# The kv product and its product with Wo, head by head on small TensorE tiles, with Wo loaded by quadrants behind the z row

## Chip, cores, metric

One core of one Trainium2 chip. The metric is the device time of the whole program in microseconds (us). A program runs several times on one chip, in turns with the kernel before; medians are quoted, and every ratio is the mean time of one kernel's fast runs over that of the other's fast runs of the same rounds, so it is not quite the ratio of the medians. The runs of one kernel in one group span 0.6 to 2.8 us here, mostly 1 to 2. The effects below are of that size, so each one is also read from the trace, in stretches of a few us, where times repeat to hundredths (the two kv blocks take 1.79 us each in before and again in b_plus64).

Names in the profile: PE is TensorE's matmul, PEld its weight load (each matmul has one of its own: 4083 of each in before), DVE is VectorE, ACT ScalarE, SPq the queue of SyncE that issues the transfers. All instructions carry the line of one helper, L176, so pieces are told apart by their tiles: `ps<-g,wv` is the kv product, `ps<-wo,kvt` its product with Wo, `ps<-pk,xres` the G product before them, `ps<-mw,pqt` the attention output after them, `ps<-pqt,zsel` the denominator.

## The reference, cut

```python
def _A_ref(x, wqkv, wo):                 # x: 1 x 2048 x 1024, H = 32 heads of Dh = 32
    q, k, v = ...                        # x @ wqkv, split by heads
    phi = lambda t: jnp.where(t > 0, t + 1, jnp.exp(t)) + 1e-06
    pq, pk = (phi(q), phi(k))
    kv = jnp.einsum('bhsd,bhse->bhde', pk, v)          # one 32 x 32 block per head
    z = jnp.einsum('bhsd->bhd', pk)
    num = jnp.einsum('bhqd,bhde->bhqe', pq, kv)
    den = jnp.einsum('bhqd,bhd->bhq', pq, z)[..., None] + 1e-06
    return (num / den) ... @ wo

h = _layernorm(x) * (1 + ca) + sa        # modulation from silu(c) @ w_mod
x = x + ga * _A_ref(h, A_wqkv, A_wo)
# ... second layer norm, then the gated feed-forward block (70% of the time, untouched here)
```

The kernel never forms v. It computes G = (modulated x) transposed times phi(k), with a rank-one term that needs the z row (the sum of phi(k)); then kv transposed = Wv transposed times G per head, then M = kv times Wo per head, and the output is phi(q)/den times M.

## The kernel before: the parts touched

```python
P.dma("wo", WO[:], wov)                      # 2 MB in one transfer, ahead of everything below

def g_group(g):                              # 16 groups of 16 matmuls 128x512, five PSUM banks in turn
    ...
def g_evac(g):                               # ACT scales a row of ZB (needs the z row), DVE evicts the bank into G
    ...

def z_row():
    ...                                      # two matmuls, a copy, then out to DRAM and back, broadcast
    zw = P.dma("zw", ZDR[0].rearrange("(g p) -> g p", p=128), ZR8[0:NHG, :])
    P.wait_for("sp", [zw])
    P.dma("zr", ZB[:], ZDR[0:1, :].to_broadcast([128, D]))

def kvt_mm(half):                            # four groups of four heads
    for hl in range(4):
        hg = 4 * half + hl
        for dt in range(NDT):
            P.pe("matmul", out=PS[:, 6, hl * 128:(hl + 1) * 128], lhsT=WV[:, dt, hg * 128:(hg + 1) * 128],
                 rhs=G[:, dt, hg * 128:(hg + 1) * 128], start=(hl == 0 and dt == 0), stop=(dt == NDT - 1), ...)
    P.dve("tensor_tensor", out=KVT[:, 4 * half:4 * half + 4, :], in0=PS[:, 6, :]..., in1=MASK..., op=ALU.mult)

def m_mm(hg, banks):                         # a block-diagonal 128x128 times Wo, two halves of 512 columns
    for nh in range(2):
        ...
        P.pe("matmul", out=PS[:, bank, :], lhsT=KVT[:, hg, :], rhs=WO[:, hg, nh * 512:(nh + 1) * 512], ...)
        ...                                  # evicted to MW by ACT and DVE in turn

# order: G groups 0..10, kvt_mm(0), G 11, m_mm(0), G 12, m_mm(1), G 13, m_mm(2), G 14, m_mm(3), G 15,
# six output matmuls, kvt_mm(1), five, m_mm(4), two, m_mm(5), two, m_mm(6), one, m_mm(7), then output matmuls only
```

In each 128x128 block of `kvt_mm` only four 32x32 blocks on the diagonal are wanted; the mask throws the other twelve away, and `m_mm` multiplies by their zeros.

## Time and profile before

| | before |
|---|---|
| median of 3 runs | 831.1 us (830.98 to 831.93) |
| span of the profiled run | 829.4 us |
| TensorE busy | 823.2 us, 99% |
| kv product | 64 matmuls 128x128, two blocks of 1.79 us |
| kv with Wo | 16 matmuls 128x512, eight pairs of 0.43 us |

The chain that ended last is TensorE for 97% of the span. Listed in order of time it runs from 20.93 us for 805.88 us through nothing but matmuls. So, by this chain, only TensorE's own time counts, and a new stop of TensorE counts in full.

TensorE's groups by form (count, then busy us and mean ns of one, then idle time before):

```profile
L176 PE MATMUL ps<-wo,kvt 128*128 128x512 bf16 x16 | 4.8, 379 | 0.0
L176 PE MATMUL ps<-g,wv 128*128 128x128 bf16 x64 | 3.9, 219 | 0.0
L176 PE MATMUL ps<-pqt,zsel 128*32 128x512 bf16 x32 | 1.9, 380 | 0.0
```

The mean of 379 ns is one matmul from its start to its modelled end; successive ones overlap (they start 216 ns apart), so costs are taken from starts. TensorE's timeline around the touched pieces (start, length, count):

```profile
130.24 3.62 PE L176 MATMUL ps<-pk,xres 128*128 128x512 bf16 x16
133.79 1.91 PE L176 MATMUL ps<-pqt,zsel 128*32 128x512 bf16 x32
...
166.72 1.95 PE L176 MATMUL ps<-g,wv 128*128 128x128 bf16 x32
168.51 3.62 PE L176 MATMUL ps<-pk,xres 128*128 128x512 bf16 x16
171.96 0.59 PE L176 MATMUL ps<-wo,kvt 128*128 128x512 bf16 x2
172.40 3.62 PE L176 MATMUL ps<-pk,xres 128*128 128x512 bf16 x16
...
188.80 1.95 PE L176 MATMUL ps<-g,wv 128*128 128x128 bf16 x32
190.59 1.24 PE L176 MATMUL ps<-mw,pqt 128*128 128x512 bf16 x5
```

The kv block starts at 166.72 and the next G group at 168.51: 1.79 us for 32 matmuls, 56 ns each. A pair of kv-with-Wo matmuls takes 0.43 us (171.964 to 172.395, unrounded). Together these pieces are 2 x 1.79 + 8 x 0.43 = 7.0 us, 0.85% of the span. The denominator's 32 matmuls show what narrow tiles can do: 32 columns each, four at a time, eight rounds in 1.84 us.

The transfer queue, and ACT's first use of the z row:

```profile
131.35 1.29 SPq L176 DMA_DIRECT2D wo<-in_A_wo_dram  x1
132.68 0.53 SPq L176 DMA_DIRECT2D z_row<-zr  x1
140.08 0.33 SPq L176 DMA_DIRECT2D zb<-z_row  x1
```

```profile
144.12 1.33 ACT L176 ACTIVATE gtmp<-zb,modcol 128x512 f32<-128x512 f32 x2 [16.09 <-DMA zb<-z_row]
```

The z row's write is issued behind Wo's 2 MB, and its read back comes 7.4 us later; ACT waits until 144.12. TensorE still does not stop: it comes back to the first of its five banks at 146.0, and DVE had freed that at 145.6.

### The profile page before, as it was taken

The numbers are of one execution on the slowest core, as the hardware profiler recorded it, in microseconds if no ns is written. First come the engines' busy times: TensorE is split into PE (matmuls) and PEld (weight loads), VectorE is DVE, ScalarE is ACT, GpSimd is POOL, SyncE is SP. The second block draws the span as 40 slices with busy tenths as digits, with TensorE's granted clock in tenths as the row PEclk, the third lists the DMA queues.
The fourth block names the chain that finished last, engine by engine and source line by source line (L and its number), as shares of the span: only waits on it lengthen the run. The fifth ranks groups of instructions, "written<-read, shape, count | busy, mean of one in ns | idle before, by whom it ended". The sixth has DMA issues, their size and how long they took to land.

```text
span 829.4 us, 10017 instructions
## 1 busy us (share of the span) xinstructions
PE 823.2 (99%) x4083; PEld 378.8 (46%) x4083; DVE 312.6 (38%) x665; ACT 197.5 (24%) x336; POOL 39.9 (5%) x57
## 2 busy tenths in 40 slices
PE   8999999999999999999999999999999999999998
PEld 4544444444444444444444444444444444444444
DVE  5797986756955521121221112122111211221111
ACT  4757641323242111011111101111110111111011
POOL 1010000000130000030000003000000300000000
PEclk9999999999999999999999999999999999999999
DMA  9969656938397985700455571045557004553000
GB/s 321 287 151 231 148 159 171 201 104 304 60 256 229 276 264 158 192 25 15 124 155 150 153 185 33 16 124 153 154 151 190 26 18 123 154 152 87 0 26 26
DMA packets 199246, 119.28 MB, mean 144 GB/s; under 512 B 57881, under 2 KB 182945, under 8 KB 199201
## 3 DMA queue, kind: packets, MB, share of 16 engines
q1 hardware_dynamic: 199184, 118.65, 52.8%
q8 instruction: 32, 0.52, 0.3%
q14 instruction: 14, 0.11, 0.0%
q10 hardware_dynamic: 16, 0.00, 0.0%
HBM read 100.67 MB, written 4.33 MB: 127 GB/s over the span
## 4 chain that ended last, share of the span: by engine, by line
PE 97%; DMA 2%; SPq 1%; issue 0%; DVE 0%
PE ps L176 97%; DMA wsa<-in_w_mod_dram 2%; SPq L176 1%; DVE xres L176 0%
## 5 line engine op out<-in xcount | busy, mean ns | idle before, releaser
L176 PE MATMUL ps<-h2t,gug 128*128 128x512 bf16 x896 | 211.7, 379 | 0.0
L176 PE MATMUL ps<-h2t,guu 128*128 128x512 bf16 x896 | 211.7, 379 | 0.0
L176 DVE TENSOR_TENSOR at<-sg,ps 128x512 bf16<-128x512 bf16 x112 | 77.0, 687 | 282.8 <-PE ps L176 281.2
L176 ACT ACTIVATE sg<-ps 128x512 bf16<-128x512 f32 x112 | 66.9, 597 | 309.7 <-PE ps L176 309.7
L176 PEld LDWEIGHTS ps<-h2t,guu 128*128 128x128 bf16 x896 | 87.6, 98 | 105.7
L176 PEld LDWEIGHTS ps<-h2t,gug 128*128 128x128 bf16 x896 | 87.7, 98 | 105.5
L176 PE MATMUL ps<-wd_a,at 128*128 128x512 bf16 (+1 forms) x512 | 112.4, 377 | 0.0
L176 PE MATMUL ps<-ht,wqk 128*128 128x512 bf16 x512 | 111.7, 379 | 0.0
L176 PE MATMUL ps<-wd_b,at 128*128 128x512 bf16 (+1 forms) x384 | 85.0, 377 | 0.0
L176 PEld LDWEIGHTS ps<-wd_a,at 128*128 128x128 bf16 x512 | 50.1, 98 | 59.6
L176 DVE TENSOR_TENSOR ut<-att,gb_b 128x512 bf16<-128x512 bf16 (+1 forms) x32 | 14.3, 447 | 166.8 <-ACT att L176 166.8
L176 PEld LDWEIGHTS ps<-ht,wqk 128*128 128x128 bf16 x512 | 49.5, 98 | 58.7 <-DVE biasq L176 0.2
L176 ACT ACTIVATE att<-ps 128x512 bf16<-128x512 f32 (+1 forms) x32 | 17.4, 591 | 182.1 <-PE ps L176 182.1
L176 PEld LDWEIGHTS ps<-wd_b,at 128*128 128x128 bf16 x384 | 37.6, 98 | 44.7
L176 PE MATMUL ps<-pk,xres 128*128 128x512 bf16 x256 | 56.5, 379 | 0.0
L176 PE MATMUL ps<-mw,pqt 128*128 128x512 bf16 x256 | 56.3, 379 | 0.0
L176 POOL TENSOR_SCALAR h2t<-h2t,modcol 128x512 bf16<-128x512 bf16 x32 | 26.3, 836 | 383.4 <-DMA h2t<-xn 383.4
L176 ACT ACTIVATE e<-ps 128x512 bf16<-128x512 f32 x56 | 33.1, 603 | 31.7 <-PE ps L176 19.8
L176 PEld LDWEIGHTS ps<-mw,pqt 128*128 128x128 bf16 x256 | 24.9, 98 | 30.2 <-DVE xres L176 0.4
L176 PEld LDWEIGHTS ps<-pk,xres 128*128 128x128 bf16 x256 | 24.9, 98 | 29.9 <-issue 0.4
L176 ACT ACTIVATE junk<-xres 128x1024 bf16<-128x1024 bf16 x24 | 25.4, 1058 | 35.1 <-DVE xres L176 34.9
L176 DVE SCALAR_TENSOR_TENSOR xres<-ps,xres 128x512 bf16<-128x512 f32 x32 | 21.4, 688 | 12.3 <-PE ps L176 11.5
(107 smaller groups left out, 344.8 us busy)
## 6 DMA issues: line engine op xcount, KB each, us to landing
gug<-in_B_w_gate_dram SPq DMA_DIRECT2D x56, 512.0 KB, 4.0
guu<-in_B_w_up_dram SPq DMA_DIRECT2D x56, 512.0 KB, 5.3
xres<-in_A_x_dram SPq DMA_DIRECT2D x20, 256.0 KB, 7.7
rb<-recip_den SPq DMA_DIRECT2D x8, 512.0 KB, 11.5
stgx<-in_w_mod_dram SPq DMA_DIRECT2D x2, 2048.0 KB, 7.9
wd_a<-in_B_w_down_dram SPq DMA_DIRECT2D x4, 1024.0 KB, 7.8
out_dram<-xres SPq DMA_DIRECT2D x31, 128.0 KB, 1.7
xres<-in_A_x_dram SPq DMA_DIRECT2D x3, 1024.0 KB, 14.1
```

The lines of the kernel that those rows point to most:

```text
L176: return getattr(e, method)(**kw)
```

## The change

Its intent is to compute only the wanted blocks. A head's kv is a matmul with 32 columns of weights, so four heads (one of each group) are put side by side in four column tiles, as the denominator's matmuls are in before, where four start 3 to 4 ns apart and the next four 206 to 216 ns later. kv with Wo needs 32 rows and 32 columns, so 16 heads are put in sixteen 32 by 32 tiles: group g takes row tile g and PSUM bank g, head h takes column tile h. For that, the change lays Wo's rows in another order in SBUF, with eight transfers (two groups of four quadrants, no waits between the four). They are issued behind the z row. The eviction of kv needs no mask. In numbers: 64 matmuls become 256, 16 become 64.

```diff
-        wov = A_wo.rearrange("(kt p) n -> p kt n", p=128)
+        wov = A_wo.rearrange("(f g h e) n -> f g e h n", f=2, g=4, h=4)
-        P.dma("wo", WO[:], wov)
+        def wo_load(f):
+            outs = [WO[32 * g:32 * g + 32, 4 * f:4 * f + 4, :] for g in range(4)]
+            def fn(e, outs=outs, f=f):
+                return [e.dma_start(out=o_, in_=wov[f, g]) for g, o_ in enumerate(outs)]
+            P.add("sp", fn, reads=[], writes=outs, lane="wo%d" % f, ninc=4, tag="wo")
...
         def kvt_mm(half):
+            for h in range(4):
                 for dt in range(NDT):
+                    for g in range(4):
+                        c0 = 512 * half + 128 * g + 32 * h
+                        P.pe("matmul", out=PS[32 * g:32 * g + 32, 6, 32 * h:32 * h + 32], lhsT=WV[:, dt, c0:c0 + 32],
+                             rhs=G[:, dt, c0:c0 + 32], start=(h == 0 and dt == 0), stop=(dt == NDT - 1), ...)
+            P.dve("tensor_copy", out=KVT[:, half, :], in_=PS[:, 6, 0:128])
+
+        def m_mm(half, nh, banks):
+            for k in range(4):
+                for g in range(4):
+                    h = (g + k) % 4
+                    P.pe("matmul", out=PS[32 * h:32 * h + 32, banks[g], :],
+                         lhsT=KVT[32 * g:32 * g + 32, half, 32 * h:32 * h + 32],
+                         rhs=WO[32 * g:32 * g + 32, 4 * half + h, nh * 512:(nh + 1) * 512], ...)
+            # four evictions to MW, two on ACT and two on DVE
...
             if g == 0:
                 z_row()
+                for f in range(2):
+                    wo_load(f)
...
-            if 11 <= g < 15:
-                m_mm(g - 11, [MB, 7])
+            if 11 <= g < 13:
+                m_mm(0, g - 11, [MB, 7, G_BANKS[4], 6])
...
         kvt_mm(1)
         wo_part(0, 1, range(2, 4))
-        # three output matmuls, m_mm(4), two, m_mm(5), two, m_mm(6), one, m_mm(7)      [summarised]
+        wo_part(1, 0, range(1))
+        m_mm(1, 0, [4, 5, 7, 6])
+        wo_part(1, 0, range(1, 4))
+        wo_part(1, 1, range(4))
+        m_mm(1, 1, [4, 5, 7, 6])
```

Left out: the smaller KVT tile, one G group moved to another bank, and the order of the first two row tiles of the output.

## The prediction

> **What bounds it now.** TensorE. The chain of waits runs through TensorE without a gap from 20.9 to 826.8 us (97% of the span); granted clock 1.0. Only TensorE time can be gained. The groups by form show the two touched pieces: `ps<-g,wv` 64 matmuls 128x128, `ps<-wo,kvt` 16 matmuls 128x512. In the timeline of TensorE the two kv blocks start at 166.72 and 188.80 and last 1.79 us each (32 at 56 ns); the kv-with-Wo matmuls come in eight pairs of 0.43 us (216 ns each), 3.45 us in all. Together 7.0 us: the ceiling.

> **What changes.** Only a 32 by 32 block per head is useful; the rest was masked. After: 256 matmuls of N=32 in four column tiles, 64 of N=512 in sixteen 32 by 32 tiles.

> The trace has a model: the denominator's 32 matmuls, 32 columns wide, N=512, at 133.79 us. Each four start 3 to 4 ns apart and the next four 206 to 216 ns later: four tiles for one streaming time [...]. Entering and leaving costs: the last full-array matmul starts 309 ns before the first tiled one, and 312 ns pass at the end, against 216: about 0.1 us each way [...].

> Estimates from these:
> - kv: 64 rounds of four. N=1 load-and-matmul pairs (the modulation columns) follow every 25 ns here; eight instructions at 3.4 ns are 27 ns. At 28 ns a round a block takes 0.9 + 0.2 us of switching, not 1.79: saves 0.7, twice = 1.4 us.
> - kv with Wo: a block of 16 tiles takes about 0.216 + 0.07 of issue + 0.2 switching = 0.5 us, not 0.86 (four full matmuls): saves 0.36, four times = 1.45 us.
> - New waits: the second half's second block reuses all four banks after 7 matmuls (1.5 us), while each of ACT and DVE has two evictions (0.60 and 0.69 us) plus latency: 0.1 to 0.2 us lost. The KVT copy before the third block (0.3 us) is about covered by three matmuls (0.65 us).

> **Off the critical path.** The z row now goes before Wo's 2 MB: before, its broadcast was issued at 140.1 (7 us after its write, queued behind Wo) and ACT waited for it until 144.1. I expect it near 137. G's evictions then start right after the reciprocal (about 141.6, not 144.9); TensorE did not wait there, so this gains 0. Wo in eight 256 KB loads lands near 145 to 148; the fold by the gate needs it at 150. The reciprocals may be a microsecond or two late; DVE has that to spare.

> **Sum.** 831.1 - 2.7 = 828.4 us; range 826.8 to 830.4. Faster by over 2%: 0.01; within 2%: 0.98; slower: 0.01.

> **What would show it.** kv blocks of about 1.1 us from start to the next full-array matmul; kv-with-Wo blocks of about 0.5 us; TensorE still without idle time between 126 and 200 us except a few tenths before the last block; `zb` landing before 140.

> **What would make it wrong.** If small matmuls on different column tiles do not overlap, and each pair costs 25 ns, a kv block (128 pairs) takes 3.2 us and the kernel gets about 1.5 us slower. If sixteen tiles writing four banks do not run at once, the Wo gain vanishes. Switching rows and columns could cost more than 0.1 us. If Wo or the reciprocals land microseconds late, DVE delays kv and TensorE idles.

## More of the kernel before

The page's chain of waits (by engine, then by line) and its line of queue 8:

```profile
PE 97%; DMA 2%; SPq 1%; issue 0%; DVE 0%
q8 instruction: 32, 0.52, 0.3%
```

## The result and the profile after

| | before | after |
|---|---|---|
| median | 831.41 us (4 runs) | 829.94 us (4 runs, 829.23 to 830.76) |
| ratio of fast runs | | 0.9982, 95% interval 0.9965 to 1.0 |
| span of the profiled run | 829.4 us | 827.4 us |

The gain is 1.5 us where 2.7 were predicted. The interval reaches 1.0, so the time alone would not settle that there is a gain; a second group (after_again, below) has 0.9984, with 0.9971 to 0.9998. The measured time lies inside the predicted range, but over a microsecond of the expected gain is missing. In this trace 79 of the 4323 matmul records are missing (their weight loads are all there), which breaks the chain of waits into 206 pieces; the timeline is read instead, with the weight loads where a matmul is missing.

The groups by form, then TensorE's timeline over the same stretch:

```profile
L176 PE MATMUL ps<-g,wv 128*32 128x32 bf16 x256 | 2.5, 182 | 0.0
L176 PE MATMUL ps<-wo,kvt 32*32 32x512 bf16 x64 | 1.7, 385 | 0.0
```

```profile
187.11 1.19 PE L176 MATMUL ps<-g,wv 128*32 128x32 bf16 x128
188.47 0.59 PE L176 MATMUL ps<-mw,pqt 128*128 128x512 bf16 x2 [0.16 <-issue]
188.99 0.43 PE L176 MATMUL ps<-wo,kvt 32*32 32x512 bf16 x16
189.36 1.68 PE L176 MATMUL ps<-mw,pqt 128*128 128x512 bf16 x7
190.97 0.43 PE L176 MATMUL ps<-wo,kvt 32*32 32x512 bf16 x16
191.34 1.04 PE L176 MATMUL ps<-mw,pqt 128*128 128x512 bf16 x4
193.41 2.96 PE L176 MATMUL ps<-mw,pqt 128*128 128x512 bf16 x12 [1.03 <-issue]
```

Both products got cheaper as planned: a kv-with-Wo block takes 191.34 - 190.97 = 0.37 us and the switch into it 0.09 more. But after the last of them TensorE makes four matmuls, and then stops for a microsecond. The releaser named is "issue", which means that the profile shows nothing that it waited for. (The 0.16 at 188.47 is a matmul whose record is missing.) The weight loads, of which none is missing, give the stop exactly, with the spacing to the one before:

```
weight load 1370 (counting from 0)   191.999 us   +0.216
weight load 1371                     193.407 us   +1.408     no semaphore on it
weight load 1372                     193.622 us   +0.215
```

The matmul of load 1370 already waits: its record starts at 193.406, so the stop lies between a weight load and its own matmul. So 1.408 - 0.216 = 1.19 us are lost in the one place. Without it the change would have gained about 2.6 us.

The transfer queue, ACT, and queue 8:

```profile
130.71 1.16 SPq L176 DMA_DIRECT2D z_row<-zr  x1
133.46 0.33 SPq L176 DMA_DIRECT2D zb<-z_row  x1
133.83 4.33 SPq L902 DMA_DIRECT2D wo<-in_A_wo_dram  x8
```

```profile
138.17 1.33 ACT L176 ACTIVATE gtmp<-zb,modcol 128x512 f32<-128x512 f32 x2 [10.68 <-DMA zb<-z_row]
q8 instruction: 34, 0.56, 0.3%
```

- **Theory A, instruction supply.** TensorE reached the seam between two blocks before the second had arrived. (That the second is asked for at about the time when TensorE enters the first was the author's assumption here.)
- **Theory B, a data wait** on ACT or DVE that the profile does not name. The first residual addition on DVE ended at 193.42, just as TensorE resumed.
- **Theory C, something that follows the change of tile mode.**

By A, a seam lies at a fixed count of instructions from the start of the program. B and C are tied to a place in the work. That makes them easy to tell apart: shift the work against the count.

### The profile page after: what moved, and what is told of

It is laid out like the page before. It is cut to its first block, busy times and chain, and to the rows that moved or that the text cites. A ratio compares the mean times of both kernels' runs of the same rounds, so it can differ in the third digit from the quotient of the medians.

```text
span 827.4 us, 10429 instructions
## 1 busy us (share of the span) xinstructions
PE 816.5 (99%) x4244; PEld 376.4 (45%) x4323; DVE 311.3 (38%) x665; ACT 197.4 (24%) x336; POOL 39.8 (5%) x57
## 4 chain that ended last, share of the span: by engine, by line
PE 96%; DVE 2%; issue 1%; DMA 0%; ACT 0%; DVEq 0%; ACTq 0%
PE ps L176 96%; DVE acc L176 1%; DMA xres<-in_A_x_dram 0%; DVE stats L176 0%; DVE pkt L176 0%; DVE e L176 0%; ACT xres L176 0%; DVE pqt L176 0%; ACT e L176 0%; DVE mv L176 0%; DVE xres L176 0%; DVE ht L176 0%; DVE ve L176 0%; DVE nmr L176 0%; DVEq L247 0%
```

## The experiments

Eleven runs were made in three groups (after_again and best_again repeat a kernel); a group shares its chip and its runs of the kernel before. All gave the right result except quiet_dma, which is wrong.

| run | median us | before, same chip | ratio, 95% interval | where TensorE stopped |
|---|---|---|---|---|
| a_plus64 | 828.94 | 831.55 | 0.9970 (0.9958 to 0.9983) | nowhere |
| a_plus16 | 833.41 | 831.55 | 1.0020 (1.0006 to 1.0034) | loads 1115 and 1371 |
| half0 | 829.82 | 831.55 | 0.9980 (0.9968 to 0.9993) | nowhere |
| b_plus64 | 832.75 | 831.55 | 1.0013 (1.0001 to 1.0026) | G, for the z row |
| after_again | 829.79 | 831.23 | 0.9984 (0.9971 to 0.9998) | load 1371 |
| z_first | 831.49 | 831.23 | 1.0004 (0.9991 to 1.0016) | nowhere |
| half1 | 834.57 | 831.23 | 1.0035 (1.0023 to 1.0048) | load 1243 |
| kv_only | 830.34 | 831.23 | 0.9990 (0.9977 to 1.0002) | nowhere |
| best_again | 828.76 | 831.57 | 0.9969 (0.9956 to 0.9981) | nowhere |
| best_wo_first | 834.97 | 831.57 | 1.0046 (1.0032 to 1.0059) | G, for the z row |
| quiet_dma | 829.33 (one run) | 831.57 | none | load 1115 |

Timed runs were five for each but quiet_dma, all in the fast state; quiet_dma has one look of unknown state.

### a_plus64: the work shifted by 64 pairs

```diff
-        warm(13, bank=3)
+        for _ in range(77):
+            P.pe("matmul", out=PS[:, 3, 0:86], lhsT=IDENT[:], rhs=E1[:, 0, 0:86], start=True, stop=True)
```

These are filler matmuls at the start of the kernel (its helper is named `warm`), there before and after the change; 77 short ones stream as many columns as the 13 long ones (6622 and 6656). In the trace of after the 13 start 426 to 427 ns apart (401 at the first step, 357 at the last), and the five of the same shape that follow from 8.66 us start 215 to 216 ns apart.

> The kernel after, with the 13 clock-warming matmuls of 512 columns at the start replaced by 77 of 86 columns: the same streaming, 64 more load-and-matmul pairs ahead of everything, so all later instructions lie half a 16 KB instruction block further on. Theory A (TensorE's instruction stream ran dry at 192.2 us after the kv block had used 256 instructions in 1.1 us; the stall sits at the seam of two fetched blocks, the 1371st weight load): the seam leaves the critical place, the 1.2 us gap is gone from the profile, and the time is about 1.2 us below after, near 828.8 us, ratio to before 0.9965 to 0.9972. Theory B (the gap is a wait for data of ACT or DVE that the profile does not name, such as the first residual addition, which ended as TensorE resumed): the program is the same from there on, the gap stays at the same matmul with about 1.2 us, time as after, ratio 0.998. Theory C (a delay that follows the change of tile mode): as B.

Measured: 828.94 us, ratio 0.9970, and no stop. TensorE's timeline at the same place:

```profile
191.55 0.43 PE L176 MATMUL ps<-wo,kvt 32*32 32x512 bf16 x16
191.92 1.25 PE L176 MATMUL ps<-mw,pqt 128*128 128x512 bf16 x5
```

The weight loads run on at 0.216 us through the place where the gap was. Theories B and C do not expect this: the work, its waits and its tile modes are the same here. (In the control b_plus64, below, some transfers ran a microsecond later with the new warming, so it is a_plus16 and half1 that put B and C out.) This trace has all its matmuls, so the true prices are read from it, each from the end of the last full matmul's 216 ns to the start of the next full one:

| block | before | a_plus64 | saved |
|---|---|---|---|
| first kv block | 1.79 us | 1.29 us | 0.50 |
| second kv block | 1.79 us | 1.22 us | 0.57 |
| kv with Wo, each of four | 0.86 us (two pairs) | 0.46 us | 0.40 |
| sum | | | 2.67 |

The time gained is 831.55 - 828.94 = 2.61 us, so the sum closes, and more closely than the noise of the runs would lead one to expect.

### a_plus16: shifted the wrong way

The same edit with 29 matmuls of 229 columns.

> The same with 29 warming matmuls of 229 columns: 16 more pairs. Theory A: the seam stays at the 1371st weight load, which is now 16 loads earlier in the program, inside the last kv-with-Wo block, reached 1.1 us earlier, while its fetch is asked for at most 0.2 us earlier: a gap of about 2 us, at another matmul than in after; time 0.7 to 1.0 us above after, about 830.8 us, ratio to before 0.999 to 1.0. Theories B and C: the gap at the same matmul of the program, 1.2 us, ratio 0.998.

Measured: 833.41 us, and the stop is at weight load 1371 again, though that is now in the middle of the last kv-with-Wo block:

```profile
190.53 1.68 PE L176 MATMUL ps<-mw,pqt 128*128 128x512 bf16 x7
192.14 0.39 PE L176 MATMUL ps<-wo,kvt 32*32 32x512 bf16 x4
194.70 0.49 PE L176 MATMUL ps<-wo,kvt 32*32 32x512 bf16 x12 [2.17 <-issue]
195.12 1.46 PE L176 MATMUL ps<-mw,pqt 128*128 128x512 bf16 x3
```

Sixteen independent matmuls are cut after the record of the fourth. Loads are 2.55 us apart where 3 ns is usual. The place by count stayed, the place in the work moved, as A alone says. The time missed the expectation of about 830.8 us. Two things were not expected: a second stop of 0.76 us at load 1115, just 256 loads earlier, in the first half's first kv-with-Wo block; and a slow clock after the long stop, with matmuls 427 ns apart in place of 216 for some eight of them, 1.6 us more (the mean granted clock of this execution is 0.998, in after 1.0). With those the time adds up: 828.8 (after without a stop) + 2.5 + 0.8 + 1.6 = 833.7.

### half0 and half1: one half of the heads each

The change applied to the first half alone and to the second half alone; the other half has its matmuls, Wo layout and order of before.

```diff
+            if f == 1:                       # half0; f == 0 in half1
+                P.dma("wof", WO[:, 4 * f:4 * f + 4, :], wof[:, 4 * f:4 * f + 4, :])
+                return
...
-        kvt_mm(1)                            # half0
+        kvt_full(1)                          # and its order of before; half1 does so for half 0
```

> The change for the first half of the heads only; the second half has its 128 by 128 matmuls, Wo layout and order of before. From the trace of after, the first half's kv block saves about 0.47 us and its two kv-with-Wo blocks 0.40 us each: 1.27 us. Theory A: no burst in the second half, no gap: 1.2 to 1.3 us below before, about 830.1 us, ratio 0.9985, so as good as or little worse than the whole change. Theory B: the gap belongs to the order of the second half (two tiles of rows taken together), which is undone, so it predicts the same here; C: a gap of some tenths may follow the first half's blocks.

Measured for half0: ratio 0.9980, 1.7 us below before, no stop. The trace has the kv block at 1.29 and the two kv-with-Wo blocks at 0.46 us, as in a_plus64. Half of the change is worth as much as the whole as it was made.

> The change for the second half of the heads only, the first half as before. By the sum of parts without stalls it saves 0.56 + 0.8 = 1.36 us. Theory A: the seams of instruction blocks lay at weight loads 1115 and 1371 (a_plus16), so one lies at 1243; here it falls into the last kv-with-Wo block (loads 1230 to 1245), 167 loads after the kv block's start at 1076, of which 128 run in 1.1 us: a gap of 2 to 2.6 us there, likely with a slow clock after it as in a_plus16, and a time of 1 to 3 us ABOVE before, so 832.5 to 834.5 us. Theories B and C (data wait, mode switching) expect the gain of 1.36 less about 1.2: ratio 0.9998.

Measured for half1: 834.57 us, 3.3 us ABOVE before, and the stop exactly where the count puts it, at weight load 1243:

```profile
193.05 0.42 PE L176 MATMUL ps<-wo,kvs 32*32 32x512 bf16 x12
196.23 0.40 PE L176 MATMUL ps<-wo,kvs 32*32 32x512 bf16 x4 [2.76 <-issue]
```

The loads are 3.15 us apart, a longer stop than the 2 to 2.6 us expected, and the matmuls after it are again 427 ns apart for some microseconds (mean granted clock 0.998). This was the hardest test of A, because by the work alone half1 should have gained 1.36 us. The seams found so far, 1115, 1243 and 1371, are 128 loads apart: one block of 256 instructions each.

### b_plus64: a control that moved

The kernel before with the warming of a_plus64.

> Control: the kernel before with the same 77 short warming matmuls. Before has no gap, and its kv blocks use 64 instructions in 1.8 us, so all theories expect ratio 1.000, within 0.0005, and no gap; if it moves by more, the warming itself changed the time and a_plus64 has to be read against this one.

Measured: 1.0013, 1.2 us slower. TensorE stopped in the G groups:

```profile
146.70 4.49 PE L176 MATMUL ps<-pk,xres 128*128 128x512 bf16 x20 [0.49 <-DVE g L176]
```

Here the z row's read back was issued at 141.14, one us later than in before, so DVE's first eviction came too late for the sixth G group; 0.66 us were lost between the first G group and the first kv block (40.70 us from load to load, before 40.04). The margin of 0.4 us that before had at this place was that thin. Why the transfers run a microsecond later with the other warming was not followed up. For a_plus64 the control means that the new warming gives nothing by itself.

### z_first: the order of the transfers alone

```diff
-        P.dma("wo", WO[:], wov)
...
             if g == 0:
                 z_row()
+                P.dma("wo", WO[:], wov)
```

> Before with one edit: Wo's single 2 MB load issued behind the z row. b_plus64 showed that the late z row can stop TensorE (its sixth G group waited for DVE's first eviction, 0.65 us lost between the first G group and the first kv block), while the profiled execution of before had 0.4 us to spare there. My prediction said the reorder gains 0: then ratio 1.000. The rival, that many executions of before lose some tenths there, expects 0.2 to 0.7 us below before, ratio 0.9992 to 0.9997 or less. The z row's broadcast should land near 138 us in either case, not 144.

Measured: 1.0004 with an interval of 0.9991 to 1.0016, the z row read back at 134.13 in place of 140.08. The order alone is worth nothing that these runs show, as predicted.

### best_wo_first: the order undone in the version without a stop

```diff
             if g == 0:                       # a_plus64, with the two lines exchanged
-                z_row()
                 for f in range(2):
                     wo_load(f)
+                z_row()
```

> a_plus64 with Wo's eight loads issued ahead of the z row, as before had its single one. The z row's broadcast then lands near 144 to 146 us in place of 140. If the reorder protects TensorE, the sixth G group waits for the first eviction by some tenths of a us (b_plus64: 0.65), time 0.3 to 1.0 us above best_again. If the reorder is idle, as z_first on the kernel before suggested (ratio 1.0004), the same time as best_again within 0.3 us.

Measured: 834.97 us, 6.2 us above best_again. The expectation had the direction and missed the size by far. The transfer queue, then TensorE:

```profile
131.84 5.89 SPq L903 DMA_DIRECT2D wo<-in_A_wo_dram  x8
137.77 0.33 SPq L176 DMA_DIRECT2D z_row<-zr  x1
144.63 0.36 SPq L176 DMA_DIRECT2D zb<-z_row  x1
```

```profile
150.19 1.03 PE L176 MATMUL ps<-pk,xres 128*128 128x512 bf16 x2 [4.56 <-DVE g L176]
```

Eight issues take 5.9 us of the queue where the single one took 1.3, so the z row is written at 137.8, then waits 7 us as in before, and TensorE stops for 4.6 us, and some ten matmuls after it start about 0.42 us apart where 0.216 is usual (mean granted clock 0.996). So the reorder is not idle in this change. It gains nothing on the kernel before (1.0004), but in a_plus64 it is what makes eight small loads affordable (6.2 us).

### after_again: is the stop an accident?

The kernel after, unchanged.

> The kernel after, unchanged, on the chip of the next three. Theory A (instruction supply) says the gap is part of the program and not an accident of one execution: again at the 1371st weight load, 1.0 to 1.5 us long, ratio to before 0.998. If the gap were an accident of one profiled execution, this profile would lack it or have it elsewhere.

Measured: ratio 0.9984, a stop at weight load 1371 again, loads 1.70 us apart, so 1.48 us lost in this execution. The matmuls after it start 0.216 us apart, where those after the 2.55 us of a_plus16 were 427 ns apart; one execution each.

### kv_only: the kv product alone

```diff
             for hl in range(4):              # in the kernel before
                 for dt in range(NDT):
-                    P.pe("matmul", out=PS[:, 6, hl * 128:(hl + 1) * 128], lhsT=WV[:, dt, hg * 128:(hg + 1) * 128], ...)
+                    for h in range(4):
+                        c0 = 512 * half + 128 * hl + 32 * h
+                        o0 = 128 * hl + 32 * h
+                        P.pe("matmul", out=PS[32 * h:32 * h + 32, 6, o0:o0 + 32], lhsT=WV[:, dt, c0:c0 + 32],
+                             rhs=G[:, dt, c0:c0 + 32], ...)
```

> Before with only the kv product on 32-column tiles (quadrant = head within its group, masked eviction, Wo and kv-with-Wo as before). The trace of after has the kv blocks at 1.32 and 1.23 us with both switches in place of 1.79, so 1.0 us less, ratio 0.9988. Theory A: the seams at loads 987, 1115, 1243, 1371 lie at least 37 loads (8 us) after the end of a kv block or inside one with its fetch asked for long before, so no gap. If kv's tiles are the part that does not pay, the ratio is 1.000 or above. What is missing from the 2.6 us of a_plus64 is then the share of kv with Wo, 1.6 us.

Measured: 830.34, 0.9 us below before, no stop. The interval reaches 1.0002, so the time alone would not settle it; the trace has the blocks cheaper by 0.5 us each, as in a_plus64. A kernel in which kv with Wo alone is tiled was not run: its tiles are written for the layout that the tiled kv product gives. Its share, 1.6 us, is read from the blocks.

### quiet_dma: why the block comes late

The kernel after with most of the data transfers between 170 and 195 us cut away.

```diff
-                P.dma("stgx1", STGX[0][:], wmv[:, :, 3072:4096])
+                P.dma("stgx1", STGX[0][:, 0:1, :], wmv[:, 0:1, 3072:4096])
-        P.dma("stgx2", STGX[1][:], wmv[:, :, 5120:6144])
+        P.dma("stgx2", STGX[1][:, 0:1, :], wmv[:, 0:1, 5120:6144])
-        for st in range(4):                  # reload of x, first four tiles
+        for st in range(1):
...                                           # and one of four tiles in each of the later reloads
```

> The kernel after with the gap, but with most of the data transfers of 170 to 195 us cut: the two modulation blocks load one of eight row blocks, the reload of x one tile of four (WRONG results on purpose; the modulation sum reads the one block eight times, so DVE's work is unchanged). A1, the instruction block comes late because its transfer stands behind the data transfers: the fetch that started 3.8 and 4.2 us after the second kv block began (after, after_again) starts within 2 us, and the gap at weight load 1371 falls below 0.3 us. A2, the delay is the supply's own: fetch start and gap stay at 3.5 to 4.5 us and 1.0 to 1.5 us.

Measured: the stop at load 1371 is gone, the loads there run on at 0.216 us. The stretch from 187 to 194 us of after, then of quiet_dma (busy us of PE, PEld, DVE, ACT, POOL, then clock, share of the DMA engines, GB/s):

```profile
187.00:194.00 7.00, 5.81 (x177) 2.88 (x178) 3.48 (x7) 2.17 (x4) 0.00 (x0) 1.00 1.05 389
```

```profile
187.00:194.00 7.00, 6.79 (x182) 3.35 (x183) 3.52 (x6) 2.17 (x4) 0.00 (x0) 1.00 0.27 82
```

In after the DMA engines are full (1.05) and the fetch starts 3.8 us after the kv block; with a share of 0.27 it starts 1.4 us after (189.75 against 188.39). So, by this one look, the block is late because the core's own data transfers fill the engines that must also bring instructions. Cutting them brought one surprise: a stop of 0.88 us at seam 1115, in the first half. There the share of the DMA engines between 166 and 171 us was 1.01, against 0.65 in after, and that fetch started 4.5 us after its kv block. It is the same effect at another seam. The record shows one difference there: the first of the cut loads, `stgx`, of 256 KB, was issued at 163.03 us, where after issued its 2 MB at 170.33. That this is what filled the engines was not tested.

### All stops of this kind together

Six stops without a semaphore were seen, in five traces. Queue 8's transfers are taken from the trace's DMA records:

```
run           seam   kv block   fetch on the      fetch     TensorE    resumed less
              load   starts     DMA engines       less kv   resumed    end of fetch
after         1371   187.11     190.92 - 191.96   3.80      193.41     1.45
after_again   1371   187.63     191.84 - 192.95   4.22      194.21     1.26
a_plus16      1115   166.69     169.72 - 171.00   3.04      172.24     1.24
a_plus16      1371   188.28     192.09 - 193.20   3.81      194.70     1.50
half1         1243   189.19     193.76 - 194.87   4.57      196.23     1.36
quiet_dma     1115   166.70     171.17 - 172.28   4.47      173.59     1.31
```

Each time TensorE resumes 1.2 to 1.5 us after a 16 KB instruction transfer has ended. Each transfer begins 3 to 4.6 us after the start of a kv block. In these six cases TensorE got to the seam before these two times and the transfer's own 1.0 to 1.3 us together had passed. In after itself the first half's seam, 1115, was passed 1.42 us after its fetch had ended, without a stop: it escaped by next to nothing.

The traces also say more about the late fetch than the one look of quiet_dma. In every row the previous seam, 128 loads earlier, lies inside the kv block, and the fetch follows it. In the ten traces with a tiled kv block 18 seams lie inside one. In three the DMA engines had a share of 0.21 or less from the seam to the fetch, and the fetch started 1.0 to 1.1 us after the seam: kv_only (167.06 to 168.17), best_wo_first (174.07 to 175.12), quiet_dma (188.73 to 189.75). In the other 15 the share was 0.68 to 1.07, and the fetch started 1.4 to 4.3 us after it. The first two runs have all their transfers and right results. Their share was not changed on purpose, so they support the reading without being a test of their own.

### best_again

> a_plus64 once more, on the chip of the next two. If its gain is real, no gap in the profile and 2.5 to 2.7 us below before, ratio 0.9967 to 0.9972, against 0.9982 to 0.9984 for the change as it was made.

Measured: 828.76 us, ratio 0.9969, no stop. The version that shifts the seams takes 0.9970 and 0.9969 of before in two groups, where the change as made has 0.9982 and 0.9984. The two were not run in one group, nor on one chip, and their intervals overlap (the ten runs took 828.57 to 829.55 us, the nine of the change as made 829.23 to 830.76), so that it beats the change as made rests on the traces as well. In its two traces TensorE runs without a stop from the first G group to the end of the kv-with-Wo blocks. It is a fragile fix: 64 pairs more ahead of the kv product took the stop away, 16 pairs more (a_plus16) gave two stops.

## Why the prediction was right, and where not

- **Ceiling and bound: right.** TensorE's time alone counts (97% of the chain); 7.0 us were there to gain from, and the blocks gave 2.67. That this is so near the 2.7 predicted is partly luck: kv gave 0.33 less than predicted, kv with Wo 0.15 more, and a wait of 0.1 to 0.2 did not come.
- **Tiles run side by side: right.** The kv-with-Wo matmuls start 3 to 4 ns apart, sixteen in about 50 ns, and the block takes 0.46 us with both switches, against an estimate of 0.5. Saved 1.6 us, predicted 1.45.
- **kv blocks: mechanism right, size a little off.** 1.29 and 1.22 us against an estimate of 1.1. The "28 ns a round" is the term: in a_plus64 the first eight rounds of the second block follow each other after 25 to 27 ns, but for one of 38, and the later ones after 32 to 36, so a round of four takes 32 ns on average (34 in the first block, which has one of 125). Saved 1.07 us, predicted 1.4.
- **Switching costs about 0.1 us each way: right**, 309 to 317 ns between starts at the edges where 216 is usual, for 32-column tiles and for 32 by 32 tiles alike.
- **"0.1 to 0.2 us lost" on reused banks: wrong, harmless.** The last block starts 0.31 us after the last full matmul, which is the switch alone. The seven matmuls covered the evictions.
- **The z row "gains 0": right for the order by itself** (z_first, 1.0004). The prediction did not see that eight loads ahead of the z row would have cost 6 us, which the order avoids (best_wo_first). It landed at 138 us, within "before 140". The reciprocals came 3.3 us later, not one or two (DVE's first scaling of phi(q) starts at 161.04, before at 157.77), and as predicted TensorE did not notice.
- **"TensorE still without idle time": wrong, and this is the step that failed.** The sum lacked a term of 1.19 us in the profiled run, 1.48 in the second one: the wait for TensorE's own instructions. The prediction counted instructions only as time to issue, not as bytes to fetch, though it knew that 64 matmuls would become 256. With the term the sum is 2.67 - 1.19 = 1.48 us, and 831.41 - 829.94 = 1.47 were measured; so close a match is luck, since the interval of the ratio spans 0 to 2.9 us.

Shown by the runs: the stop is tied to the count of instructions (a_plus64, a_plus16, half1), and it ends 1.2 to 1.5 us after an instruction transfer every time. That it goes away when data transfers leave the engines free was seen in one execution (quiet_dma), and the other traces agree. Left open: at which instruction exactly a fetch is asked for, what the 1.2 to 1.5 us after the transfer are, and why b_plus64's transfers ran late.

## What to carry to other kernels

When a change replaces few large instructions by many small ones, count the instructions as bytes too: find the engine's instruction transfers in the trace, and compare how long a block lasts in the burst (here 1.1 us, in the feed-forward block 27.6) with how long a fetch takes while the data transfers of that stretch run (here, at the six stops, it began 3.0 to 4.6 us after the kv block had, took 1.0 to 1.3 us, and TensorE resumed 1.2 to 1.5 us after it). A stop of an engine that the profile puts down to nothing, at a place in the middle of independent work, can be tested in one run by putting a few dozen cheap instructions far ahead of it: here 16 pairs left the stop at weight load 1371 and so moved it against the work, which told the supply from a wait in the work. And splitting one transfer into many can cost the queue that issues them (Wo's eight took 5.9 us of it ahead of the z row, its one 1.3); put the small transfer that someone waits for in front.
